# Gate products of two groups as 64-row pairs inside a burst, with stages A and B in another order

## The chip, the cores and the metric

The kernel runs on one core of one Trainium2 chip. The metric is the time in microseconds (us) of one execution on the device. A core has TensorE (PE, matmuls; PEld is its weight loads), VectorE (DVE), ScalarE (ACT), GpSimd (POOL) and SyncE (SP), each with a queue of its own that runs in order; semaphores order them among each other.

## The reference

Two layers for x of shape 4 x 12608 x 128 in f32, with 32 inducing rows and an inner width of 1024:

```python
def mab(q, kv):
    s = scale * (q @ kv.transpose(0, 2, 1))
    s = s - s.max(-1, keepdims=True)
    a = np.exp(s)
    a /= a.sum(-1, keepdims=True) + 1e-09
    return a @ kv
h = mab(I, x)                 # 32 x 128 for each batch
x = mab(x, h)                 # back to 12608 x 128
...
x_prev = x shifted by one row
xk = mu_k * x + (1.0 - mu_k) * x_prev
xr = mu_r * x + (1.0 - mu_r) * x_prev
k = np.maximum(xk @ w_k, 0.0)
v = k * k @ w_v
r = 1.0 / (1.0 + np.exp(-(xr @ w_r)))
return r * v
```

## The kernel before

The second attention ends in `a @ h`, and h has 32 rows only. So the kernel multiplies h into the weights once a batch: W is h (and h for the shifted row) times w_k, Wg the same times w_r. What goes through the big products is then R, the attention probabilities of a group of 512 rows: 32 rows for the row itself and 32 for the row before it, 64 in all. To keep f32 precision a number is split into a high and a low part; a product takes three terms (high x high, low x high, high x low). R holds both parts, and its 64 rows stand twice, in the upper and the lower half of the 128 partitions.

The work is 4 batches of 25 groups (24 of 512 rows, one of 320), and 4 units of 256 inner columns for each group: 400 steps, numbered n. The order on every engine is written out by hand:

- In each even step PE runs a burst: `up` for units n and n+1, twelve 64-row matmuls (L788) into two tiles `ps_a`. Two neighbouring matmuls use the upper and the lower 64 rows of the array.
- `square` of unit n: DVE takes the relu out of PSUM (`k_t`, L798), ACT squares it into `kh` (L803) and again into `k_t` (L804), POOL forms `kl`, the difference (L806). In the steps of the set `high_vector` DVE makes kh (L800).
- `down` of unit n-4: six 128-row matmuls (L817) into the bank `ps_v` of the group.
- `zgate` once a group, in the step of its second unit: two 128-row matmuls (L776) of Wg, whose high part lies in the upper 64 rows and whose low part lies in the lower 64, with R; then ACT's Sigmoid into `rT` (L778). The product lies in the same bank into which `down` will write v of that group.
- `gate` multiplies v with rT on DVE (L822), `store` transposes (L833) and writes out.

Between these steps stand two other stages, for which `at(n, f)` puts f at the end of step n and `soon(n, f)` puts it ahead of that step's `square`. They come in segments of 12 steps that start at s:

- Stage A, the first attention of the next batch, for one block of 2048 rows: `load_x` (1 MB to `xb`, L202), four transposes `btr` on DVE (L339) whose result SP spreads to `xt`, `scores` on PE into bank pb_a (L367), maxima, `expo` on ACT (L403, L404, result e1t), `etrans` on DVE, `hmm` on PE into pb_a (L436), `acc` on DVE.
- Stage B, the second attention of this batch, for four groups: `scores` on PE into pb_b (L617), transposes, maximum, Exp on ACT (L634), normalisation, `high` and `low` into `hl`. SP then spreads hl to the R of each group (L584, L597, L591). R has five buffers.

PSUM has eight banks: four for the two `ps_a` tiles, two for `ps_v`, and pb_a and pb_b. Sigmoid and Exp lie in two tables of ACT, and a change between them is an ACT_TABLE_LOAD. SP issues all these DMAs, in one order.

Of the kernel before, what the change touches and what calls it, by code (L numbers as in the profile page):

```python
# [19 lines left out]
def kernel(  # L20
# [38 lines left out]
    r_pool = ctx.enter_context(tc.tile_pool(name="r_pool", bufs=NR))  # L59
    mp = ctx.enter_context(tc.tile_pool(name="mp", bufs=2))  # L60
    pa = ctx.enter_context(tc.tile_pool(name="pa", bufs=2, space=bass.MemoryType.PSUM))
    pv = ctx.enter_context(tc.tile_pool(name="pv", bufs=2, space=bass.MemoryType.PSUM))
    pb = ctx.enter_context(tc.tile_pool(name="pb", bufs=1, space=bass.MemoryType.PSUM))
    banks = iter("ab" * 64)

    def pb_tile(bank=None):

# [141 lines left out]
    def stage_a_head(j):  # L209
# [32 lines left out]
                        nc.gpsimd.tensor_copy(out=S.xs[h + i][:, 1:], in_=dst[:, :G - 1])  # L242

        def scores():
            L.s1 = pv.tile([P, G], F32, name="ps_v")
            for i in range(Q):
                nc.tensor.matmul(out=L.s1[M * i:M * (i + 1), :w], lhsT=indT, rhs=S.xt[j, i][:, :w],
                                 start=True, stop=True)
# [72 lines left out]
    def stage_a(b, j, at, t):  # L321
# [131 lines left out]
            S.xb.pop(j)  # L453

        for c in range(Q):
            at(t + ((-1, 0, 1, 3) if (b, j) != (1, 0) else (4, 5, 6, 7))[c], lambda c=c: btr(c))
        if tail:
            at(t + 8, t_tr)
            soon(t + 11, t_scores)
        at(t + 9, scores)  # L460
        at(t + 10 + tail, common)
        at(t + 11 + tail, running)
        soon(t + 15, expo)
        at(t + 16, etrans)
        if tail:
            at(t + 16, t_etrans)
        at(t + 17, sums)
        at(t + 17, lambda: hmm(0))
        at(t + 17, lambda: hmm(1))
        at(t + 17, t_hmm)  # L470
        at(t + 19, acc)
        k = order_a.index((b, j))
        for bn, jn in order_a[k + 1:]:
            if jn < NBLK - 1:
                at(2 if (b, j) == (1, 0) else t + 8, lambda: load_x(bn, jn))
                if jn == NBLK - 2:
                    at(t + 8, lambda: load_x(bn, jt))
                break


    def combine(b, at=None, t=0):
# [45 lines left out]
        def hfin():  # L527
            ps = pb_tile("b")
            nc.tensor.matmul(out=ps[:, :M], lhsT=S.acc, rhs=L["sw"], start=True, stop=True)
            S.hT = sm.tile([P, M], F32, name="hT")  # L530
            nc.vector.tensor_copy(out=S.hT, in_=ps[:, :M])
            h4 = L["h4"] = sm.tile([P, Q, M], F32, name="h4", bufs=1)
            for n, mu in enumerate((muk, omuk, mur, omur)):
                nc.vector.tensor_scalar(out=h4[:, n, :], in0=ps[:, :M], scalar1=mu, scalar2=None, op0=ALU.mult)
            S.W = [wp.tile([P, F // 2], F32R, name=f"W{s}") for s in range(2)]
            S.Wg = wp.tile([P, C], F32R, name="Wg")

        def wpart(gate, tile):


            X = {}
            cw = C if gate else F // 2
            rows = slice(HP if gate else 0, P)

            def prod():
                X["ps"] = tile()[:, :cw]
                chunks = wk_sb.rearrange("p (c e d) -> p e c d", e=2, d=P)
                for n in range(Q):
                    o = X["ps"][M * n:M * (n + 1), :]
                    if not gate:  # L550
                        o = o.rearrange("m (c d) -> m c d", d=P)
                    nc.tensor.matmul(out=o, lhsT=L["h4"][:, 2 * gate + n % 2, :],  # L552
                                     rhs=wr_sb if gate else chunks[:, n // 2], start=True, stop=True)

            def high():
                nc.scalar.copy(out=(S.Wg if gate else S.W[0]), in_=X["ps"])

            def low():
                hi, lo = (S.Wg, S.Wg) if gate else S.W
                nc.vector.tensor_tensor(out=lo[rows], in0=X["ps"][rows], in1=hi.bitcast(F32)[rows],  # L560
                                        op=ALU.subtract)
            return prod, high, low

        if ahead:
# [193 lines left out]

    NG = (NBLK - 1) * Q + 1
    UB = NG * NU  # L760

    class Group:
        def __init__(self, b, g):
# [3 lines left out]
            self.ps = {}  # L767
            self.v = None

        def zgate(self):  # L770

            S, w = self.S, self.w
            R = S.R[self.g]
            ps = self.v = pv.tile([P, G], F32, name="ps_v")[:, :w]
            for s in range(2):
                nc.tensor.matmul(out=ps[:, :w], lhsT=S.Wg, rhs=R[:, s, :w], start=(s == 0), stop=(s == 1))  # L776
            self.rT = mp.tile([P, G], F32, name="rT")[:, :w]
            nc.scalar.activation(out=self.rT, in_=ps[:, :w], func=AF.Sigmoid)  # L778

        def up(self, u):  # L780

            S, w = self.S, self.w
            R = S.R[self.g]
            ps = self.ps[u] = pa.tile([P, UC, G], F32, name="ps_a")
            for n, (a, k) in enumerate(((0, 0), (1, 0), (0, 1))):
                for r in range(2):
                    rows = slice(HP * r, HP * (r + 1))
                    nc.tensor.matmul(out=ps[:, r, :w], lhsT=S.W[a][rows, u * P:(u + 1) * P],  # L788
                                     rhs=R[rows, k, :w], start=(n == 0), stop=(n == 2))
# [17 lines left out]
                                                       in1=kh.bitcast(F32)[:, :, a:z], op=ALU.subtract)  # L807

        def down(self, u):
            w = self.w  # L810
            if self.v is None:
                self.v = pv.tile([P, G], F32, name="ps_v")[:, :w]
            kh, kl = self.h.pop(u)
            for n, (wt, kk) in enumerate(((wvh, kh), (wvl, kh), (wvh, kl))):
                for c in range(UC):
                    fc = u * UC + c
                    nc.tensor.matmul(out=self.v, lhsT=wt[:, fc, :], rhs=kk[:, c, :],  # L817
                                     start=(fc == 0 and n == 0), stop=(fc == FC - 1 and n == 2))
# [5 lines left out]
        def store(self):  # L824
# [10 lines left out]
            if g % span == span - 1 or g == NG - 1:  # L835
# [126 lines left out]
    def at(n, f):  # L962
        events.setdefault(n, []).append(f)
# [3 lines left out]

    def start():

        def bank():  # L970
            return pv.tile([P, G], F32, name="ps_v")

        wk = wpart(0, bank)
        wg = wpart(1, bank)
        (sc0, df0, ex0, nm0, turn0, hi0, lo0, idle), *rest = [stage_b_first(g) for g in range(Q)]
        run([sc0, wk[0], rest[0][0], df0, ex0, wk[1], nm0, lambda: idle(1), turn0, hi0, wk[2], lo0])
        plan = ((None, None, None, at, soon, soon, at), (at,) * 4 + (soon, soon, at), (at, at, soon, at, soon, soon, at))
        steps = ((0, 0, 0, 0, 2, 2, 2), (0, 1, 1, 2, 4, 4, 4), (4, 5, 6, 7, 8, 8, 8))
        for fs, when, ns in zip(rest, plan, steps):
            for k, (f, put, n) in enumerate(zip(fs, when, ns)):  # L980
                if put is not None:
                    put(n, f)
                elif k > 0:
                    f()
        at(0, wg[0])
        at(0, wg[1])
# [6 lines left out]
    for b in range(B):  # L993
        t = b * UB + (4 if b == 0 else 0)
        for j in range(NBLK - 1):
            s = t + SEG * j
            high_vector |= {s + 4, s + 8}
            if b + 1 < B:
                stage_a(b + 1, j, at, s)
            if b or j:  # L1000
                stage_b(b, j + 1, at, s + (1 if j != (b == 0) else -3 if b else -1))
            else:
                stage_b(b, j + 1, at, 3, direct=True, early=soon, offsets=(0, 1, 1, 1, 3, 4, 4, 4, 5, 6, 7))
        if b + 1 < B:
# [10 lines left out]
    with tc.manual_schedule():  # L1015
        head()
        start()
        for n in range(len(units) + LAG + 2):
# [5 lines left out]
            if grp is None:  # L1024
                run(late)
                late = []
            else:
                if n % 2 == 0:
                    for g, v in units[n:n + 2]:
                        g.up(v)  # L1030
                run(early.pop(n, []))
                low = grp.square(u, n in high_vector)
                run(late)
                late = []
                part = grp.w - (grp.w // 2 if n >= len(units) - 3 else 0)
# [43 lines left out]
```

## Time and profile before

| | |
|---|---|
| time, three runs | 1100.82 median (1098.99 to 1100.83) us |
| the profiled execution's own time | 1100.15 us |
| its span, first to last instruction | 1098.2 us |
| mean granted TensorE clock | 0.995 |
| HBM traffic | 28.07 MB read, 25.82 MB written, 49 GB/s |

The page of the profile lists the busy time of each engine and its share of the span, the chain of work that ended last, and the groups of instructions that took most time. "busy, mean ns of one | idle before, releaser" means: total time, mean time of one instruction, and how long the engine had been idle ahead of the group, with what ended most of that.

### The profile page before, as it was taken

The page shows a single profiled execution, that of the slowest core. Times are in us where ns is not written, and L with a number is a line of the kernel's source. Part 1 is how long each engine was busy: PE and PEld are TensorE (multiplying, and loading weights), DVE is VectorE, ACT ScalarE, POOL GpSimd, SP SyncE. Part 2 cuts the span into 40 slices and gives each one's busy share as a digit, 9 for nine tenths or more (in the row PEclk, how much of TensorE's full clock was granted, in tenths as well). Part 3 has the DMA queues.
Part 4 walks back from the last instruction along what each step waited for, and adds up shares of the span by engine and source line. Part 5 has one row for each costly group of instructions (what it writes and reads, how often), then busy time and mean ns, then how long its engine had stood idle before and what let it go on. Part 6 is the DMA issues. An engine that isn't in the chain of part 4 may idle for free.

```text
span 1098.2 us, 19347 instructions
## 1 busy us (share of the span) xinstructions
PE 1071.4 (98%) x6622; PEld 736.6 (67%) x6622; DVE 911.5 (83%) x1296; ACT 961.5 (88%) x1101; POOL 947.1 (86%) x422
## 2 busy tenths in 40 slices
PE   7889999999999999999999999999999999999997
PEld 5456666666676666666676666666767667667775
DVE  4799899997788999997779899998777788887665
ACT  5487989898999898998899888989999999999995
POOL 2278988898889988989888989889888999999996
PEclk9999999999999999999999999999999999999998
DMA  9305676674156566665245746765315434433422
GB/s 276 120 5 114 159 157 163 130 167 100 27 119 163 121 161 148 136 151 121 46 81 132 173 94 152 167 145 116 72 26 116 88 60 90 94 80 68 92 36 35
DMA packets 267633, 123.59 MB, mean 113 GB/s; under 512 B 225648, under 2 KB 247056, under 8 KB 265232
## 3 DMA queue, kind: packets, MB, share of 16 engines
q1 hardware_dynamic: 267200, 122.35, 50.8%
q8 instruction: 52, 0.85, 0.3%
q14 instruction: 45, 0.37, 0.1%
q10 hardware_dynamic: 336, 0.02, 0.0%
HBM read 28.07 MB, written 25.82 MB: 49 GB/s over the span
## 4 chain that ended last, share of the span: by engine, by line
PE 89%; DVE 3%; ACT 3%; SPq 2%; issue 1%; DMA 1%; POOL 0%; DVEq 0%; ACTq 0%
PE ps_v L817 51%; PE ps_a L788 27%; PE ps_v L776 4%; PE pb_b L617 2%; PE pb_a L367 2%; PE pb_a L436 2%; DVE k_t L798 1%; ACT kh L803 1%; SPq L188 1%; SPq L95 1%; ACT k_t L804 1%; SPq L207 1%; DMA xb<-in_x_dram 1%; ACT L778 0%; PE pb_a L552 0%
## 5 line engine op out<-in xcount | busy, mean ns | idle before, releaser
L806 POOL TENSOR_TENSOR kl<-k_t,kh 128x1024 fp32r<-128x1024 f32 (+2 forms) x400 | 935.5, 2380 | 109.3 <-ACT k_t L804 102.1
L798 DVE TENSOR_SCALAR k_t<-ps_a 128x1024 f32<-128x1024 f32 (+1 forms) x400 | 477.1, 1198 | 98.2 <-PE ps_a L788 76.1
L804 ACT ACTIVATE k_t<-k_t 128x1024 f32<-128x1024 f32 (+1 forms) x400 | 417.5, 1048 | 51.7 <-DVE kh L800 18.0
L803 ACT ACTIVATE kh<-k_t 128x1024 fp32r<-128x1024 f32 (+1 forms) x352 | 365.1, 1037 | 47.5 <-DVE k_t L798 45.0
L788 PE MATMUL ps_a<-R,W 64*128 64x512 f32 (+1 forms) x2400 | 331.4, 407 | 5.2 <-DVE k_t L798 4.5
L788 PEld LDWEIGHTS ps_a<-R,W 64*128 64x128 f32 x2400 | 208.7, 184 | 126.6 <-issue 49.6
L817 PE MATMUL ps_v<-kh,wvh 128*128 128x512 f32 (+1 forms) x800 | 270.4, 419 | 2.1 <-ACT rT L778 2.1
L817 PE MATMUL ps_v<-kl,wvh 128*128 128x512 f32 (+1 forms) x800 | 248.8, 392 | 1.4 <-POOL kl L806 1.2
L817 PE MATMUL ps_v<-kh,wvl 128*128 128x512 f32 (+1 forms) x800 | 248.6, 392 | 0.0
L817 PEld LDWEIGHTS ps_v<-kh,wvh 128*128 128x128 f32 x800 | 133.8, 188 | 93.0 <-issue 48.5
L817 PEld LDWEIGHTS ps_v<-kl,wvh 128*128 128x128 f32 x800 | 149.5, 188 | 36.9 <-POOL kl L806 1.5
L817 PEld LDWEIGHTS ps_v<-kh,wvl 128*128 128x128 f32 x800 | 149.7, 188 | 34.9
L822 DVE TENSOR_TENSOR oT<-ps_v,rT 128x512 f32<-128x512 f32 (+1 forms) x100 | 66.9, 669 | 18.7 <-PE ps_v L817 18.4
L833 DVE STREAM_TRANSPOSE ot<-oT 128x512 f32<-128x512 f32 x96 | 66.9, 697 | 0.0
L776 PE MATMUL ps_v<-R,Wg 128*128 128x512 f32 (+1 forms) x200 | 63.7, 400 | 0.0
L800 DVE SCALAR_TENSOR_TENSOR kh<-ps_a,k_t 128x1024 fp32r<-128x1024 f32 x48 | 58.8, 1225 | 1.7
L778 ACT ACTIVATE rT<-ps_v 128x512 f32<-128x512 f32 (+1 forms) x100 | 57.9, 579 | 0.3
L339 DVE STREAM_TRANSPOSE xs<-xb 128x512 f32<-128x512 f32 x72 | 49.9, 693 | 0.8 <-DMA xb<-in_x_dram 0.4
L776 PEld LDWEIGHTS ps_v<-R,Wg 128*128 128x128 f32 x200 | 36.7, 189 | 8.8 <-issue 0.6
L778 ACT ACT_TABLE_LOAD x31 | 39.8, 1283 | 0.6
L617 PE MATMUL pb_b<-xt,hT 128*32 128x512 f32 x184 | 24.4, 603 | 0.3 <-DVE R L749 0.3
L663 DVE TENSOR_TENSOR hl<-pb_b,hl 128x512 fp32r<-128x512 f32 x23 | 15.8, 688 | 7.0 <-ACT hl L660 6.7
(215 smaller groups left out, 530.2 us busy)
## 6 DMA issues: line engine op xcount, KB each, us to landing
out_dram<-ot SPq DMA_DIRECT2D x184, 128.0 KB, 2.7
R<-R SPq DMA_DIRECT2D x88, 256.0 KB, 3.0
xb<-in_x_dram SPq DMA_DIRECT2D x18, 1024.0 KB, 5.4
xt<-xs SPq DMA_DIRECT2D x288, 64.0 KB, 2.0
R<-hl SPq DMA_DIRECT2D x96, 128.0 KB, 2.3
R<-hl SPq DMA_DIRECT2D x96, 127.8 KB, 2.4
kh<-in_x_dram SPq DMA_DIRECT2D x4, 512.0 KB, 8.1
kl<-in_x_dram SPq DMA_DIRECT2D x4, 512.0 KB, 7.4
```

The costliest lines, as they stand in the source:

```text
L339: nc.vector.transpose(out=xs.rearrange("p (s q) -> p s q", q=M), in_=S.xb[j][:, :, M * c:M * (c + 1)])
L776: nc.tensor.matmul(out=ps[:, :w], lhsT=S.Wg, rhs=R[:, s, :w], start=(s == 0), stop=(s == 1))
L778: nc.scalar.activation(out=self.rT, in_=ps[:, :w], func=AF.Sigmoid)
L788: nc.tensor.matmul(out=ps[:, r, :w], lhsT=S.W[a][rows, u * P:(u + 1) * P], rhs=R[rows, k, :w], start=(n == 0), stop=(n == 2))
L798: nc.vector.tensor_scalar(out=k, in0=ps, scalar1=0.0, scalar2=None, op0=ALU.max)
L800: nc.vector.scalar_tensor_tensor(out=kh, in0=ps, scalar=0.0, in1=k, op0=ALU.max, op1=ALU.mult)
L803: nc.scalar.activation(out=kh, in_=k, func=AF.Square)
L804: nc.scalar.activation(out=k, in_=k, func=AF.Square)
L806: return lambda eng, a, z: eng.tensor_tensor(out=kl[:, :, a:z], in0=k[:, :, a:z], in1=kh.bitcast(F32)[:, :, a:z], op=ALU.subtract)
L817: nc.tensor.matmul(out=self.v, lhsT=wt[:, fc, :], rhs=kk[:, c, :], start=(fc == 0 and n == 0), stop=(fc == FC - 1 and n == 2))
L822: nc.vector.tensor_tensor(out=self.oT, in0=self.v, in1=self.rT, op=ALU.mult)
L833: nc.vector.transpose(out=ot[:, o:o + w], in_=self.oT)
```

## The change

The gate products of two groups are made together. `zpair` stands in the steps n with n mod 8 = 6 from n = 14 on, behind the `up` burst, and issues six 64-row matmuls: for each of the three terms one for the first group, with the upper 64 rows, and one for the second, with the lower 64. For that Wg becomes two tiles of 128 rows, one for each part. The second matmul of a pair must write another bank than the first. The first group's product goes into the `ps_v` bank that the second group's v will use, the second group's into pb_a, or pb_b at every place where n-4 is 10 more than a segment's start (counted from the batch's start, in the first three batches). The two sigmoids come at the end of the step's work on ACT. Groups 0 and 1 keep a gate product each of its own, now with three matmuls.

Stage A and B move so that the bank is free between their own uses. In stage A the `btr` go from steps -1, 0, 1, 3 of the segment to -6, -5, -2, -1; `expo`, `etrans`, `hmm` and `acc` come two steps earlier; `load_x` goes from step 8 to step 3. Stage B always starts at s-1 (before: at s+1, with s-3 and s-1 at the starts of batches). The steps of `high_vector` change.

```diff
-        def zgate(self):
-            S, w = self.S, self.w
-            R = S.R[self.g]
-            ps = self.v = pv.tile([P, G], F32, name="ps_v")[:, :w]
-            for s in range(2):
-                nc.tensor.matmul(out=ps[:, :w], lhsT=S.Wg, rhs=R[:, s, :w], start=(s == 0), stop=(s == 1))
-            self.rT = mp.tile([P, G], F32, name="rT")[:, :w]
-            nc.scalar.activation(out=self.rT, in_=ps[:, :w], func=AF.Sigmoid)
+        def zpart(self, ps, a, k, rows, n):
+            nc.tensor.matmul(out=ps, lhsT=self.S.Wg[a][rows, :], rhs=self.S.R[self.g][rows, k, :self.w],
+                             start=(n == 0), stop=(n == len(TERMS) - 1))
+        def sigmoid(self, ps):
+            self.rT = mp.tile([P, G], F32, name="rT")[:, :self.w]
+            nc.scalar.activation(out=self.rT, in_=ps, func=AF.Sigmoid)
+        def zgate(self):
+            ps = self.bank()
+            for n, (a, k) in enumerate(TERMS):
+                self.zpart(ps, a, k, slice(0, HP), n)
+            self.sigmoid(ps)
...
+    def zpair(n, two):
+        last = two[1].b == B - 1 and two[1].g == NG - 1
+        r = n - (0 if n >= UB else 4)
+        spot = r % UB
+        side = "b" if r < (B - 1) * UB and spot < 7 * SEG and spot % SEG == SEG - 2 else "a"
+        ps = [pb_tile("b") if last else pv_tile(two[1].b * NG + two[1].g), pb_tile(side)]
+        ps = [t[:, :grp.w] for grp, t in zip(two, ps)]
+        for m, (a, k) in enumerate(TERMS):
+            for h in range(2):
+                two[h].zpart(ps[h], a, k, slice(HP * h, HP * (h + 1)), m)
+        return lambda: run([lambda grp=grp, t=t: grp.sigmoid(t) for grp, t in zip(two, ps)])
...
         for c in range(Q):
-            at(t + ((-1, 0, 1, 3) if (b, j) != (1, 0) else (4, 5, 6, 7))[c], lambda c=c: btr(c))
+            at(t + ((-6, -5, -2, -1) if b > 1 or j > 1 else (-1, 0, 1, 3) if j else (4, 5, 6, 7))[c], lambda c=c: btr(c))
...
-        soon(t + 15, expo)
-        at(t + 16, etrans)
+        soon(t + 13, expo)
+        at(t + 14, etrans)
...
-        at(t + 17, lambda: hmm(0))
-        at(t + 17, lambda: hmm(1))
+        at(t + 15, lambda: hmm(0))
+        at(t + 15, lambda: hmm(1))
...
-                at(2 if (b, j) == (1, 0) else t + 8, lambda: load_x(bn, jn))
+                at(2 if (b, j) == (1, 0) else t + 3, lambda: load_x(bn, jn))
...
-            high_vector |= {s + 4, s + 8}
+            high_vector |= {s + 2, s + (3 if (s + 2) % (2 * NU) == NU + 2 else 7)}
...
-                stage_b(b, j + 1, at, s + (1 if j != (b == 0) else -3 if b else -1))
+                stage_b(b, j + 1, at, s - 1, early=soon, offsets=(0, 1, 1, 2, 3, 5, 5, 6, 7, 7, 9))
...
+                sig = None
+                if n % (2 * NU) == NU + 2 and n > 2 * NU:
+                    sig = zpair(n, (units[n - NU - 2][0], units[n - 2][0]))
...
-                if n >= 2 * NU and u == 1:
-                    grp.zgate()
+                if sig:
+                    sig()
```

The rows below are the program's order on one engine: source line, operation, output tile <- inputs, shape, and a count where equal rows follow each other. A name's number tells one use of a buffer from the next.

PE before, in the two steps at whose end stage A's `hmm` stands: the gate product is between the two `down`, in the bank of its own group.

```order
L817 MATMUL ps_v_4624<-kh_4595,wvh_111 128x512 x2
L817 MATMUL ps_v_4624<-kh_4595,wvl_112 128x512 x2
L817 MATMUL ps_v_4624<-kl_4596,wvh_111 128x512 x2
L776 MATMUL ps_v_4753<-R_4198,Wg_3481 128x512 x2
L817 MATMUL ps_v_4624<-kh_4618,wvh_111 128x512 x2
L817 MATMUL ps_v_4624<-kh_4618,wvl_112 128x512 x2
L817 MATMUL ps_v_4624<-kl_4619,wvh_111 128x512 x2
L436 MATMUL pb_a_4770<-xb_4110,e1_4743 32x128 x16
```

PE in the changed kernel, steps 126 and 127, from the last row of the burst to `hmm`.

```order
L803 MATMUL ps_a_4728<-R_4269,W0_3509 128x512 x2
L781 MATMUL ps_v1_4735<-R_4241,Wg0_3511 128x512
L781 MATMUL pb_a_4736<-R_4269,Wg0_3511 128x512
L781 MATMUL ps_v1_4735<-R_4241,Wg1_3512 128x512
L781 MATMUL pb_a_4736<-R_4269,Wg1_3512 128x512
L781 MATMUL ps_v1_4735<-R_4241,Wg0_3511 128x512
L781 MATMUL pb_a_4736<-R_4269,Wg0_3511 128x512
L830 MATMUL ps_v0_4688<-kh_4606,wvh_111 128x512 x2
L830 MATMUL ps_v0_4688<-kh_4606,wvl_112 128x512 x2
L830 MATMUL ps_v0_4688<-kl_4607,wvh_111 128x512 x2
...
L441 MATMUL pb_a_4777<-xb_4026,e1_4761 32x128 x16
```

The gate products have moved out of the `down` stretch into the burst, and one of them lies in pb_a, which is the bank of `hmm` too.

ACT before, around the same place: stage A's Exp (L403, L404), the squares of the steps, stage B's Exp (L634), and the sigmoid.

```order
L403 ACT_TABLE_LOAD
L403 ACTIVATE alpha_4686<-mkr_4177,nb_4562 128x1
L404 ACTIVATE e1t_4684,ss_4685<-pb_a_4508,nb_4562 128x512
L803 ACTIVATE kh_4690<-k_t_4689 128x1024
L804 ACTIVATE k_t_4689<-k_t_4689 128x1024
L804 ACTIVATE k_t_4730<-k_t_4730 128x1024
L634 ACTIVATE s2_4681<-s2_4681 128x512
L803 ACTIVATE kh_4747<-k_t_4746 128x1024
L804 ACTIVATE k_t_4746<-k_t_4746 128x1024
L778 ACT_TABLE_LOAD
L778 ACTIVATE rT_4756<-ps_v_4753 128x512
```

ACT in the changed kernel, steps 125 to 127.

```order
L408 ACT_TABLE_LOAD
L408 ACTIVATE alpha_4701<-mkr_4239,nb_4647 128x1
L409 ACTIVATE e1t_4699,ss_4700<-pb_a_4580,nb_4647 128x512
L818 ACTIVATE kh_4705<-k_t_4704 128x1024
L819 ACTIVATE k_t_4704<-k_t_4704 128x1024
L637 ACTIVATE s2_4696<-s2_4696 128x512
L819 ACTIVATE k_t_4744<-k_t_4744 128x1024
L786 ACT_TABLE_LOAD
L786 ACTIVATE rT_4751<-ps_v1_4735 128x512
L786 ACTIVATE rT_4753<-pb_a_4736 128x512
```

Between stage A's Exp and the sigmoids one pair of squares less stands there than before, and two sigmoids follow each other.

SP before, at a load of x: the spread of one group (L584, L597), the load (L202), the output (L840).

```order
L591 DMA R_5081<-R_5081 64x1024
L584 DMA R_5208<-hl_4866 32x2x1
L597 DMA R_5208<-hl_4866 32x1024
L597 DMA R_5208<-hl_4866 32x2x511
L202 DMA xb_5243<-in_x_dram 128x2048
L840 DMA out_0_dram<-ot_5136 32x32x32 x4
L591 DMA R_5208<-R_5208 64x1024
```

SP in the changed kernel, step 139.

```order
L594 DMA R_5038<-R_5038 64x1024
L587 DMA R_5172<-hl_4883 32x2x1
L600 DMA R_5172<-hl_4883 32x1024
L600 DMA R_5172<-hl_4883 32x2x511
L207 DMA xb_5176<-in_x_dram 128x2048
L594 DMA R_5172<-R_5172 64x1024
L347 DMA xt_5272<-xs_5276 32x512
```

The load again stands behind a spread, but the transposes whose results SP spreads (L347) now follow it directly.

More of the change, by code (lines that the diff above doesn't have):

```diff
@@ L61, with pv_tile @@
     pa = ctx.enter_context(tc.tile_pool(name="pa", bufs=2, space=bass.MemoryType.PSUM))
-    pv = ctx.enter_context(tc.tile_pool(name="pv", bufs=2, space=bass.MemoryType.PSUM))
+    pv = ctx.enter_context(tc.tile_pool(name="pv", bufs=1, space=bass.MemoryType.PSUM))
     pb = ctx.enter_context(tc.tile_pool(name="pb", bufs=1, space=bass.MemoryType.PSUM))
     banks = iter("ab" * 64)
+    sides = iter((0, 1) * 16)
+    def pv_tile(side=None):
+        return pv.tile([P, G], F32, name=f"ps_v{next(sides) if side is None else side % 2}")
     def pb_tile(bank=None):
@@ L244, in scores @@
         def scores():
-            L.s1 = pv.tile([P, G], F32, name="ps_v")
+            L.s1 = pv_tile()
             for i in range(Q):
@@ L462, in stage_a @@
         at(t + 11 + tail, running)
-        soon(t + 15, expo)
-        at(t + 16, etrans)
+        soon(t + 13, expo)
+        at(t + 14, etrans)
         if tail:
-            at(t + 16, t_etrans)
-        at(t + 17, sums)
-        at(t + 17, lambda: hmm(0))
-        at(t + 17, lambda: hmm(1))
-        at(t + 17, t_hmm)
-        at(t + 19, acc)
+            at(t + 14, t_etrans)
+        at(t + 15, sums)
+        at(t + 15, lambda: hmm(0))
+        at(t + 15, lambda: hmm(1))
+        at(t + 15, t_hmm)
+        at(t + 17, acc)
         k = order_a.index((b, j))
@@ L535, in hfin @@
             S.W = [wp.tile([P, F // 2], F32R, name=f"W{s}") for s in range(2)]
-            S.Wg = wp.tile([P, C], F32R, name="Wg")
+            S.Wg = [wp.tile([P, C], F32R, name=f"Wg{s}") for s in range(2)]
         def wpart(gate, tile):
@@ L542, in wpart @@
             cw = C if gate else F // 2
-            rows = slice(HP if gate else 0, P)
             def prod():
@@ L555, in high @@
             def high():
-                nc.scalar.copy(out=(S.Wg if gate else S.W[0]), in_=X["ps"])
+                nc.scalar.copy(out=(S.Wg if gate else S.W)[0], in_=X["ps"])
             def low():
-                hi, lo = (S.Wg, S.Wg) if gate else S.W
-                nc.vector.tensor_tensor(out=lo[rows], in0=X["ps"][rows], in1=hi.bitcast(F32)[rows],
-                                        op=ALU.subtract)
+                hi, lo = S.Wg if gate else S.W
+                nc.vector.tensor_tensor(out=lo, in0=X["ps"], in1=hi.bitcast(F32), op=ALU.subtract)
             return prod, high, low
@@ L760 @@
     UB = NG * NU
+    TERMS = ((0, 0), (1, 0), (0, 1))
     class Group:
@@ L768, in __init__, with bank @@
             self.v = None
-        def zgate(self):
-            S, w = self.S, self.w
-            R = S.R[self.g]
-            ps = self.v = pv.tile([P, G], F32, name="ps_v")[:, :w]
-            for s in range(2):
-                nc.tensor.matmul(out=ps[:, :w], lhsT=S.Wg, rhs=R[:, s, :w], start=(s == 0), stop=(s == 1))
-            self.rT = mp.tile([P, G], F32, name="rT")[:, :w]
-            nc.scalar.activation(out=self.rT, in_=ps[:, :w], func=AF.Sigmoid)
+        def bank(self):
+            if self.v is None:
+                self.v = pv_tile(self.b * NG + self.g)[:, :self.w]
+            return self.v
+        def zpart(self, ps, a, k, rows, n):
[4 more added lines that the diff above has]
+            nc.scalar.activation(out=self.rT, in_=ps, func=AF.Sigmoid)
+        def zgate(self):
+            ps = self.bank()
+            for n, (a, k) in enumerate(TERMS):
+                self.zpart(ps, a, k, slice(0, HP), n)
+            self.sigmoid(ps)
         def up(self, u):
@@ L784, in up @@
             ps = self.ps[u] = pa.tile([P, UC, G], F32, name="ps_a")
-            for n, (a, k) in enumerate(((0, 0), (1, 0), (0, 1))):
+            for n, (a, k) in enumerate(TERMS):
                 for r in range(2):
@@ L809, in down @@
         def down(self, u):
-            w = self.w
-            if self.v is None:
-                self.v = pv.tile([P, G], F32, name="ps_v")[:, :w]
+            self.bank()
             kh, kl = self.h.pop(u)
@@ L968, in start @@
     def start():
[L970 to L974, printed above, removed]
+        wk = wpart(0, pv_tile)
+        wg = wpart(1, pv_tile)
         (sc0, df0, ex0, nm0, turn0, hi0, lo0, idle), *rest = [stage_b_first(g) for g in range(Q)]
```

## The prediction

> **What bounds the kernel now.** I read the page's busy times first, then the chain that ended last, then the costliest groups.
>
> ```profile
> PE 1071.4 (98%) x6622; PEld 736.6 (67%) x6622; DVE 911.5 (83%) x1296; ACT 961.5 (88%) x1101; POOL 947.1 (86%) x422
> PE 89%; DVE 3%; ACT 3%; SPq 2%; issue 1%; DMA 1%; POOL 0%; DVEq 0%; ACTq 0%
> L776 PE MATMUL ps_v<-R,Wg 128*128 128x512 f32 (+1 forms) x200 | 63.7, 400 | 0.0
> xb<-in_x_dram SPq DMA_DIRECT2D x18, 1024.0 KB, 5.4
> ```
>
> PE is busy 98% of the span and carries 89% of the chain; the 200 gate products are a PE group of their own. But ACT, POOL and DVE are at 83 to 88%. The next view, busy time by windows (us, then PE, PEld, DVE, ACT, POOL with counts, the granted clock, DMA share), shows the steady state and three windows of the start.
>
> ```profile
> 371.00:403.00 32.00, 32.00 (x200) 21.68 (x200) 29.92 (x43) 28.81 (x33) 28.44 (x13) 1.00 0.51 107
> 55.00:60.00 5.00, 3.59 (x27) 2.26 (x24) 4.38 (x8) 4.13 (x7) 3.42 (x2) 0.73 0.00 0
> 60.00:65.00 5.00, 4.25 (x30) 1.89 (x32) 4.36 (x8) 4.94 (x6) 3.69 (x2) 0.93 0.00 0
> ```
>
> In steady state PE never stops while ACT, at 28.81 of 32 us, has only a tenth to spare. So a PE slot saved is time saved, and work on ACT that PE is made to wait for is time lost. The timeline of PE gives the price of a slot.
>
> ```profile
> 387.50 1.67 PE L788 MATMUL ps_a<-R,W 64*128 64x512 f32 x12
> ...
> 392.10 1.66 PE L788 MATMUL ps_a<-R,W 64*128 64x512 f32 x12
> 393.69 0.73 PE L817 MATMUL ps_v<-kh,wvh 128*128 128x512 f32 x2
> ...
> 394.73 0.63 PE L817 MATMUL ps_v<-kl,wvh 128*128 128x512 f32 x2
> 395.19 0.63 PE L776 MATMUL ps_v<-R,Wg 128*128 128x512 f32 x2
> 395.66 0.63 PE L817 MATMUL ps_v<-kh,wvh 128*128 128x512 f32 x2
> ...
> 397.15 1.08 PE L436 MATMUL pb_a<-xb,e 128*32 128x128 f32 x32
> 398.16 1.67 PE L788 MATMUL ps_a<-R,W 64*128 64x512 f32 x12
> ```
>
> From burst to burst a pair of steps takes 4.60 us (387.50 to 392.10). Two 128-row matmuls advance PE by 0.47 (395.19 to 395.66), so a slot is 0.233. The burst's twelve 64-row matmuls advance it by 1.59 (392.10 to 393.69): six slots, 1.40, and 0.19 for the change of shape. So two 64-row matmuls on the two halves of the rows share one slot. Stage A's sum, `hmm`, takes 1.0 (397.15 to 398.16).
>
> **1. The pairs on PE.** A pair issues six 64-row matmuls, three slots, in place of four: 0.233 saved. It stands behind the burst in the same shape, so no change of shape is added. Of 49 pairs, 45 save 0.233 and four with a 320-column group about 0.06 (such a matmul taken at 320/512 of a slot): 10.7. Groups 0 and 1 go alone with three matmuls for two: +0.47. Together **-10.2**. LDWEIGHTS (21.68 of 32 us) run beside PE.
>
> **2. `hmm` behind the second sigmoid.** At nine places (n = 30, 54, 78, 126, 150, 174, 214, 238, 262) a pair and stage A's `hmm` fall into one pair of steps, and both write pb_a. The pair's product in pb_a must wait until Exp has read stage A's scores there, and `hmm`, at the end of step n+1, until the second sigmoid has read the product. Both are work of ACT. Its rows at such a place before, in the order that stays:
>
> ```profile
> 389.84 1.06 ACT L803 ACTIVATE kh<-k_t 128x1024 fp32r<-128x1024 f32 x1 [0.47 <-DVE k_t L798]
> 391.00 1.06 ACT L804 ACTIVATE k_t<-k_t 128x1024 f32<-128x1024 f32 x1
> 392.08 1.28 ACT L403 ACT_TABLE_LOAD   x1
> 393.37 0.29 ACT L403 ACTIVATE alpha<-mkr,nb 128x1 f32<-128x1 f32 x1
> 393.57 0.67 ACT L404 ACTIVATE e1t<-pb_a,nb 128x512 f32<-128x512 f32 x1
> 394.24 1.04 ACT L803 ACTIVATE kh<-k_t 128x1024 fp32r<-128x1024 f32 x1
> 395.37 2.25 ACT L804 ACTIVATE k_t<-k_t 128x1024 f32<-128x1024 f32 x2
> 397.53 0.61 ACT L634 ACTIVATE s<-s 128x512 f32<-128x512 f32 x1
> ...
> 400.52 1.28 ACT L778 ACT_TABLE_LOAD   x1
> 401.82 0.60 ACT L778 ACTIVATE rT<-ps_v 128x512 f32<-128x512 f32 x1
> ```
>
> Let T0 be the start of the burst of step n-2 (387.50 here). ACT takes kh of that step at T0+2.34, when DVE's relu has come, and is then busy without a gap: kh 1.16, k 1.08, table load 1.29, alpha 0.20, e1t 0.67 (ends T0+6.74), kh 1.13, k 1.08, stage B's Exp 0.65, k 1.08 (its kh is on DVE), table load 1.30, and the two sigmoids 0.49 and 0.60: the second ends at T0+13.1. PE gets to the product at T0+4.60+1.40 = 6.00 and waits 0.74 for e1t. Without any wait it would be at `hmm` at T0+2x4.60+0.70 = 9.90. It stands there until 13.1: 3.2 us a place in all, the 0.74 within it, **+28.5**. Before, nobody waited for the sigmoid (its bank was read next by the gate); that was its cover. The bounds are nought, if ACT ran ahead by that much, and 9x4.5 = 40 if a 1.3 us table load more came in. I take the chain, since each link is a row and ACT has no gap in it.
>
> **3. Stage B's scores behind the second sigmoid.** Where the product is in pb_b (n = 14, 38, 62, 110, 134, 158, 222, 246), B's scores follow at the end of step n+1. The sigmoid ends 2.34+1.16+1.08+0.49+0.60 = 5.67 after the step's burst starts; PE is there at 4.60+0.70 = 5.30: 0.4 each. At n = 86 and 182 the scores are in the same step and wait about 0.9. Together **+4.8** (0 to 10).
>
> **4. The x block behind a later spread.** SP issues everything in order. Its rows and waits:
>
> ```profile
> 405.91 0.53 SPq L202 DMA_DIRECT2D xb<-in_x_dram  x1
> 406.54 0.64 SPq L584 DMA_DIRECT2D R<-R  x1
> 412.40 1.22 SPq L597 DMA_DIRECT2D R<-hl  x2
> SPq L584 <- PE ps_a L788: 45.5, 18, 5.3
> ```
>
> With five R buffers, the spread of group f waits for the last matmul that reads R of group f-5, and already did so for up to 5.3 us. That was `up` at step 4(f-5)+2; for an even f-5 it is now the pair's product at 4(f-5)+6. SP is blocked there, and all behind it. At n = 43, 139, 227 and 251 the load of x, now at s+3, stands behind such a spread, and the first transpose, now at six steps before the next segment, needs it. From the burst T3 of that step: product ends T3+2.4, three issues (0.64+1.22) to T3+4.3, landing 5.4, T3+9.7. Then DVE, in order:
>
> ```profile
> 392.20 0.70 DVE L339 STREAM_TRANSPOSE xs<-xb 128x512 f32<-128x512 f32 x1
> ...
> 394.00 1.21 DVE L798 TENSOR_SCALAR k_t<-ps_a 128x1024 f32<-128x1024 f32 x1
> 395.24 1.23 DVE L800 SCALAR_TENSOR_TENSOR kh<-ps_a,k_t 128x1024 fp32r<-128x1024 f32 x1
> ```
>
> Behind the transpose (0.62 to the next start) are the relu of the next step (1.24) and its kh on DVE (1.14): T3+12.7. The second half of the next burst writes the PSUM tile that this kh reads, and PE is there at T3+5.30+0.80 = 6.1. It waits 6.6 us, four times: **+26.4**. The bounds are nought, if the spread is not what holds the load, and 4x8 = 32 with a landing at 6.8. I take 6.6: the wait on R is in the row above already. Elsewhere the load waits for `hmm` alone and lands about 1.5 us before its transpose, so I cost it at nothing; it is covered by those 1.5 us.
>
> **5. The clock.** The chip's start shows what idle PE can cost: in the windows above the granted clock is 0.73 and 0.93, after this wait:
>
> ```profile
> 56.74 1.22 PE L788 MATMUL ps_a<-R,W 64*128 64x512 f32 x6 [1.41 <-DVE k_t L798]
> 35.00:40.00 5.00, 3.34 (x61) 1.61 (x53) 3.68 (x15) 2.70 (x9) 0.48 (x2) 1.00 0.00 0
> ```
>
> The loss is 5x0.27+5x0.07 = 1.7 us. A window with as much idle time (1.66 of 5 us, in pieces) kept 1.00, so not every wait does it. I take one such loss for each of the four long waits, **+6.8** (0, to 13 losses, 22). The Trainium skill (TensorE: Matmul & The Clock Gate, Part 1: The HAM clock gate) says that the clock halves after at least one idle free-running window of about 3.4 us. By that rule waits of 3.2 us or less never fill a window and those of 6.6 may; an estimate from that page is up to 3.4 us at half clock, 1.7 each, the same sum. The row speaks against it as far as it goes: there the clock fell after 1.41 us idle, so the short waits could trigger it too.
>
> The other moves (stage A's Exp and transposes two to five steps earlier, `acc`, which steps have kh on DVE) leave the counts on every engine as they were; table loads are as many as before. They fill the same 29.92 of 32 us on DVE, and I cost them at nothing; without that cover a DVE operation of 0.7 us at each of 18 segments would be 13.
>
> **The sum.** -10.2 + 28.5 + 4.8 + 26.4 + 6.8 = +56.3. On the profiled execution (1100.15, of which 1098.2 is the span) that gives 1156.4; the median shown is 0.7 above it, so **1157**.
>
> **The rivals.** (a) The blocked loads cost nothing, since the spread is released earlier or DVE has time: -26.4-6.8, 1123.5. For it: the longest wait of a spread was 5.3 us and hurt nobody. Against: the load moves from behind two segments' slack to six steps ahead of its use. (b) The clock falls after all 13 waits: 9x1.7 = 15 more, 1172. For it the row with 1.41 us; against it the window that kept 1.00. (c) The other side: ACT is ahead. ACT's tenth to spare gathers between the places, PE's waits are covered, and only the slots count: 1100.8-10.2 = 1090.6. It decides once the waits total under 10.2 us, that is, under 0.8 at each of 13 places, for which ACT would have to end its sigmoid 2.4 us sooner. Against it: ACT cannot start before DVE's relu of the same burst (the row with 0.47 idle), so what it has to spare cannot be saved up. (d) No change: gains and waits cancel within 0.2% (2.2 us, about the least that a measurement of this kernel tells from no change); only by accident.
>
> **How the numbers follow.** The full sum, with terms 2 to 4 each off by up to a third (1140 to 1168): 0.58. Rival (a), 1116 to 1132: 0.17. Rival (b): 0.06. Between 1103 and 1116, half of term 2 only: 0.04. Rival (c): 0.12. Same: 0.03. The full sum and (a) hold 0.75 between 1116 and 1168; with the upper part of the half case and the lower edge of (b), 1110 to 1170 holds about 0.79. Faster 0.12, same 0.03, slower 0.85.
>
> **What would show it.** Profile after: the gate products as 300 matmuls with 64 rows on PE (step 1); PE idle ahead of `hmm` for ACT's second rT, and ahead of the product in pb_a for e1t (step 2); ahead of B's scores for rT (3); SP waiting at the spread for a product, DVE's transpose idle for the DMA of xb, then PE's burst idle for DVE's kh (4); windows with a clock below 1.00 (5). The prediction is wrong if PE's idle time ahead of `hmm` is under 1 us a place, or if no transpose waits for xb.

## The result and the profile after

The changed kernel takes 1197.1 us against 1100.0 in the same runs: a ratio of 1.0874 (95% interval 1.0852 to 1.0895). One of the four executions behind this median took 2011.0 us and stands outside the ratio; the median of the other three is 1196.0. The direction was forecast and the size was not: +56 forecast, +97 measured, above the range.

Busy times and the chain of the page, after:

```profile
PE 1094.1 (91%) x6722; PEld 739.6 (62%) x6722; DVE 908.6 (76%) x1296; ACT 967.3 (81%) x1101; POOL 947.9 (79%) x422
PE 54%; ACT 14%; DVE 13%; issue 7%; DMA 4%; SPq 2%; POOL 1%; DVEq 0%; ACTq 0%
```

DVE, ACT and POOL are busy as long as before, to within 6 us. PE's share of the chain fell from 89 to 54%. PE's idle time is 1196.5-1094.1 = 102.4 us, before 1098.2-1071.4 = 26.8: 75.6 more. Its busy time grew by 22.7, though each pair saves a slot. So the 98.3 us that the span grew by are waits and slower matmuls. PE's waits by what ended them (us in total, times, longest):

```profile
PE ps_a L803 <- DVE kh L815: 38.7, 9, 7.4
PE pb_a L441 <- ACT rT L786: 19.6, 9, 2.9
PE pb_a L781 <- ACT e1t L409: 4.6, 9, 0.9
PE pb_b L620 <- ACT rT L786: 3.3, 10, 0.8
```

None of these four is in the list of before. They are the waits of the prediction's steps 4, 2, 2 and 3; the counts of 9 and 10 are those of steps 2 and 3, and the first came nine times where step 4 had four. On SP, the spread's waits were 45.5 us for `up` before; now the list has, for the pair's product:

```profile
SPq L587 <- PE pb_a L781: 159.9, 25, 11.7
```

**A pair and `hmm` on one bank** (n = 30), timelines of PE and ACT:

```profile
144.07 1.67 PE L803 MATMUL ps_a<-R,W 64*128 64x512 f32 x12
...
146.36 0.49 PE L781 MATMUL pb_a<-R,Wg 64*128 64x512 f32 x1 [0.39 <-ACT e1t L409]
...
147.25 0.73 PE L830 MATMUL ps_v<-kh,wvh 128*128 128x512 f32 x2
...
152.33 1.30 PE L441 MATMUL pb_a<-xb,e 128*32 128x128 f32 x32 [2.01 <-ACT rT L786]
```

```profile
145.55 0.67 ACT L409 ACTIVATE e1t<-pb_a,nb 128x512 f32<-128x512 f32 x1
...
149.90 1.28 ACT L786 ACT_TABLE_LOAD   x1
151.19 0.60 ACT L786 ACTIVATE rT<-ps_v 128x512 f32<-128x512 f32 x1
151.68 0.59 ACT L786 ACTIVATE rT<-pb_a 128x512 f32<-128x512 f32 x1
```

ACT ends the second sigmoid at 152.27, and 0.06 later PE starts `hmm`. The burst that T0 names began at 139.48, so the sigmoid ends at T0+12.8 (forecast 13.1).

**The load of x behind a spread** (n = 43 to 49): SP, DVE, PE.

```profile
193.35 0.67 SPq L587 DMA_DIRECT2D R<-hl  x1
194.07 1.27 SPq L600 DMA_DIRECT2D R<-hl  x2
195.38 0.58 SPq L207 DMA_DIRECT2D xb<-in_x_dram  x1
```

```profile
201.05 0.71 DVE L344 STREAM_TRANSPOSE xs<-xb 128x512 f32<-128x512 f32 x1 [6.96 <-issue]
201.69 1.19 DVE L813 TENSOR_SCALAR k_t<-ps_a 128x1024 f32<-128x1024 f32 x1
202.98 1.23 DVE L815 SCALAR_TENSOR_TENSOR kh<-ps_a,k_t 128x1024 fp32r<-128x1024 f32 x1
```

```profile
190.96 1.66 PE L803 MATMUL ps_a<-R,W 64*128 64x512 f32 x12
192.46 0.39 PE L781 MATMUL ps_v<-R,Wg 64*128 64x512 f32 x1
...
193.26 0.73 PE L830 MATMUL ps_v<-kh,wvh 128*128 128x512 f32 x2
...
196.26 0.96 PE L803 MATMUL ps_a<-R,W 64*128 64x512 f32 x6
204.26 1.65 PE L803 MATMUL ps_a<-R,W 64*128 64x512 f32 x6 [7.04 <-DVE kh L815]
```

The pair of step 46 starts at 192.46, the spread goes out at 193.35, the load at 195.38; the transpose starts at 201.05 after 6.96 us of DVE idle, and PE's second half of the burst stands for 7.04. The profile names no releaser for the transpose ("issue"); a load lands 5.6 us after its issue in the median, which is 201.0 here. The same rows show the price of a pair: from burst to burst 190.96 to 196.26 is 5.30, that is 0.70 above the 4.60 without one, as forecast.

### The profile page after: what moved, and what is told of

The parts are those of the page before. It is cut to its first block, busy times and chain, and to the rows that moved or that the text cites. A ratio compares the mean times of both kernels' runs of the same rounds, so it can differ in the third digit from the quotient of the medians.

```text
span 1196.5 us, 19640 instructions
## 1 busy us (share of the span) xinstructions
PE 1094.1 (91%) x6722; PEld 739.6 (62%) x6722; DVE 908.6 (76%) x1296; ACT 967.3 (81%) x1101; POOL 947.9 (79%) x422
## 4 chain that ended last, share of the span: by engine, by line
PE 54%; ACT 14%; DVE 13%; issue 7%; DMA 4%; SPq 2%; POOL 1%; DVEq 0%; ACTq 0%
PE ps_v L830 30%; PE ps_a L803 18%; DVE k_t L813 8%; ACT kh L818 4%; ACT k_t L819 4%; DMA xb<-in_x_dram 3%; PE pb_b L620 2%; ACT rT L786 2%; PE pb_a L441 1%; ACT L786 1%; PE pb_a L372 1%; DVE kh L815 1%; PE ps_v L781 1%; DVE xs L344 1%; ACT e1t L409 1%
## 5 line engine op out<-in xcount | busy, mean ns | idle before, releaser
L803 PE MATMUL ps_a<-R,W 64*128 64x512 f32 (+1 forms) x2400 | 346.1, 417 | 48.3 <-DVE kh L815 38.7
L803 PEld LDWEIGHTS ps_a<-R,W 64*128 64x128 f32 x2400 | 213.0, 190 | 179.3 <-issue 46.5
L830 PE MATMUL ps_v<-kh,wvh 128*128 128x512 f32 (+1 forms) x800 | 275.4, 426 | 3.2 <-ACT rT L786 2.9
L830 PE MATMUL ps_v<-kh,wvl 128*128 128x512 f32 (+1 forms) x800 | 252.2, 397 | 0.0
L830 PEld LDWEIGHTS ps_v<-kl,wvh 128*128 128x128 f32 x800 | 151.9, 191 | 35.7
L781 PE MATMUL ps_v<-R,Wg 64*128 64x512 f32 (+1 forms) x150 | 45.5, 398 | 0.0
L441 PE MATMUL pb_a<-xb,e 128*32 128x128 f32 x576 | 20.4, 284 | 20.4 <-ACT rT L786 19.6
L781 PE MATMUL pb_a<-R,Wg 64*128 64x512 f32 (+1 forms) x114 | 33.0, 396 | 4.6 <-ACT e1t L409 4.6
L441 PEld LDWEIGHTS pb_a<-xb,e 128*32 128x32 f32 x576 | 14.8, 110 | 27.7 <-ACT rT L786 23.5
L375 DVE TENSOR_REDUCE mx<-pb_a 128x1 f32<-128x512 f32 x18 | 12.4, 691 | 24.6 <-PE pb_a L372 24.2
```

What stands on the lines that cost most here:

```text
L781: nc.tensor.matmul(out=ps, lhsT=self.S.Wg[a][rows, :], rhs=self.S.R[self.g][rows, k, :self.w], start=(n == 0), stop=(n == len(TERMS) - 1))
```

## Experiments

Ratios are to the kernel before, with 95% intervals. Where no other kernel is named, the diff is against the changed kernel.

| kernel | us | ratio |
|---|---|---|
| e1, spreads behind the pair | 1156.8 | 1.0509 (1.0491 to 1.0527) |
| e2, transposes back | 1155.7 | 1.0503 (1.0476 to 1.0530) |
| e3, no second product at nine places | 1168.8 | 1.0632 (1.0598 to 1.0666) |
| e4, order alone | 1123.0 | 1.0205 (1.0190 to 1.0220) |
| e5, sigmoids first | 1178.3 | 1.0720 (1.0689 to 1.0752) |
| e6, order, transposes back | 1120.8 | 1.0194 (1.0176 to 1.0211) |
| e7, bank free | 1139.7 | 1.0363 (1.0347 to 1.0380) |
| e8, bank free, sigmoids first | 1127.9 | 1.0249 (1.0235 to 1.0263) |
| e9, balanced | 1105.2 | 1.0047 (1.0031 to 1.0063) |
| e10, order, balanced | 1157.7 | 1.0517 (1.0500 to 1.0533) |
| e11, order, one switch | 1142.8 | 1.0394 (1.0377 to 1.0412) |
| e12, order, both Exps in a step | 1137.5 | 1.0340 (1.0315 to 1.0365) |
| e13, order, Exp apart | 1097.8 | 0.9989 (0.9977 to 1.0000) |

**e1: is it the spread that holds the load?**

```diff
-            s = max(first + ..., NU * (f - NR) + 3 + (0 if full else i))
+            free = NU * (f - NR) + (3 if (f - NR) % 2 or f - NR < 2 else 7)
+            s = max(first + ..., free + (0 if full else i))
```

> The changed kernel with the spread of a group that reuses the R buffer of the first group of a pair put four steps later, behind that pair's product. Theory (a spread in front of the load of x waits for the pair): the four waits of 7.2 to 7.6 us at n = 48, 144, 232, 256 shrink to the 2 us that the other late loads show, 4x5.4 = 21.6, and part of the lost clock with it, about 5: 1170 (1163 to 1180). Rival (SP is behind with its own issues, the spread's wait matters little): 1190 or more.

Measured 1156.8, 40 us less than the changed kernel. PE's waits:

```profile
PE pb_a L441 <- ACT rT L787: 19.5, 9, 2.9
PE ps_a L804 <- DVE kh L816: 10.3, 5, 4.3
```

The four long waits are gone, not merely shortened to 2 us, and so are those of 1.92 and 1.71 us at n = 60 and 244; the wait at n = 24 grew from 3.27 to 4.30. The clock came back in part (0.975 to 0.986), and the time is below the expected range. The wait at `hmm` is untouched. The rival is out.

**e2: only the transposes at their old steps.**

```diff
-            at(t + ((-6, -5, -2, -1) if b > 1 or j > 1 else (-1, 0, 1, 3) if j else (4, 5, 6, 7))[c], ...
+            at(t + ((-1, 0, 1, 3) if (b, j) != (1, 0) else (4, 5, 6, 7))[c], ...
```

> The changed kernel with only the four transposes of each x block back at the old steps (-1, 0, 1, 3 of the segment in place of -6, -5, -2, -1). Theory (DVE's first transpose waits for the block, and PE for DVE): all ten waits of PE ahead of the second half of a burst go, 45 us, with some 12 us of lost clock; the waits for the sigmoid stay: 1140 (1133 to 1148). Rival (DVE is crowded by the new order of stage B, and PE waits for its relus): the transposes fall on stage B's steps now, 1165 or more.

Measured 1155.7, between the two forecasts. The waits for x go, but DVE's work, crowded, brings new ones:

```profile
PE pb_a L441 <- ACT rT L786: 21.5, 9, 2.9
PE pb_a L441 <- DVE e L420: 5.0, 6, 0.8
...
PE ps_a L803 <- DVE kh L815: 2.9, 2, 1.5
```

Both theories hold in part: 36 us of waits for kh went, and 4 for DVE's e came (5.0 against 0.8).

**e3: the nine second products left out** (the second group's gate is taken from the first group's product there).

> The changed kernel, which at the nine places where the pair and hmm both use pb_a leaves the second group's product out and takes its sigmoid from the first group's product; the two sigmoids stay. Theory (PE waits there for ACT to read the bank): 21 + 9 us of waits go, some 8 us of lost clock, and 4 us at n = 60 and 244 where the load waited for a late hmm: 1155 (1148 to 1165). Rival (the wait only moves, to DVE's transpose or the gate): 1180 or more.

```profile
PE ps_a L803 <- DVE kh L815: 39.4, 9, 9.3
PE ps_a L803 <- DVE k_t L813: 11.6, 12, 3.9
PE ps_v L830 <- ACT rT L786: 7.5, 11, 1.5
```

Measured 1168.8; the profiled execution took 1175.2. Both pb_a waits are gone, as the theory says, but the gain is 28 us and not 42. The waits at n = 60 and 244, which the theory put down to a late `hmm`, did not go: they grew from 1.92 to 3.89 and from 1.71 to 3.00, and that at n = 144 from 7.45 to 9.29. Those for relu and rT grew as well. So the wait at `hmm` had been cover for later ones.

**e5: the sigmoids ahead of the step's squares**, the one line `sig()` moved up.

> The changed kernel with the two sigmoids of a pair ahead of the squares of their step on ACT in place of behind them; nothing else. Theory (PE stands at hmm for ACT's order of work): each sigmoid ends one square (1.06 us) sooner where kh is on DVE, two where it is on ACT, so 9x1.06 at hmm and the 4.2 us ahead of stage B's scores go, with some lost clock; the waits for x stay: 1182 (1175 to 1189). Rival (PE waits for something else that ends with the sigmoid): 1194 or more.

```profile
PE pb_a L441 <- ACT rT L786: 8.7, 9, 1.1
```

Measured 1178.3, in the range. The wait at `hmm` fell from 19.6 to 8.7, 1.2 a place, for one square taken out of its way (forecast 1.06); the wait ahead of stage B's scores is no longer listed. It is ACT's order that PE stands for.

**e4, e6: the new order with the old gate products.** e4 is the kernel before with the change's steps; e6 has the transposes back as well.

> The kernel before with only the new order of stages A and B (steps, high_vector, load of x) and its old gate products. Theory (the order costs only where a load of x is late, and without pairs no spread holds it for long): six to ten waits of about 2 us, some lost clock: 1118 (1106 to 1130). Rival (the order as such is the loss, the pairs cost nothing): 1170 or more.

> The kernel before with the new order of stages A and B, but with the transposes of x at their old steps. Theory (the order costs by late loads of x alone): as before, 1101 (1098 to 1105). Rival (the new steps of stage B and of kh on DVE crowd DVE): 1108 or more.

e4 lies in its range and e6 does not: with the transposes back it is 2 us faster and not 22. PE's waits for kh fell from 12.4 to 6.7, and 6.1 for DVE's e came. I had missed that without pairs the old sigmoid at s+1 falls between the two Exps of a segment. The groups of ACT in e4:

```profile
L778 ACT ACT_TABLE_LOAD x46 | 59.0, 1283 | 0.8
L634 ACT ACT_TABLE_LOAD x27 | 34.6, 1283 | 0.5
```

The sigmoid's line has 46 table loads, where it had 31 before, and stage B's Exp 27, where it had 13. Neither kernel is a clean test of the order.

**e10, e11, e12: three attempts at a clean one, each with a wait of its own.**

> The kernel before with the new order of stages A and B, old gate products, the same spread of DVE's work as e9_balanced, and each sigmoid one step later, so that it falls behind both Exps of a segment (without that the new order has 92 table loads in the program in place of 62, as e4 and e6 have). Theory (the order costs by DVE's crowding, late loads and those table loads only): 1101 (1098 to 1106). Rival (the new steps of stage B cost in themselves): 1112 or more.

> The kernel of e4_order_alone with each sigmoid one step later, which takes its 30 additional table loads away (38 us of ACT); transposes, loads and kh on DVE as the change has them. Theory (e4's 22 us are late loads and DVE): 1117 (1110 to 1122). Rival (they are ACT's table loads): 1106 or less.

> The kernel before, old gate products and sigmoids where they were; stage B two steps earlier as in the change, the spread of DVE's work of e9_balanced, and stage A's Exp in the step of stage B's Exp, so that the table loads stay at 62. Theory (stage B's place as such costs nothing; what e4, e6, e10 and e11 lost is late loads, DVE, table loads and the sigmoids that e10 and e11 put late): 1101 (1098 to 1105). Rival (B at s-1 costs in itself): 1110 or more. With it, e9 says what the pairs are worth when nothing waits for them: theory, e9 within 5 us of this.

The waits of PE that decide, of e10 and of e12:

```profile
PE ps_v L822 <- ACT rT L783: 44.5, 30, 3.7
```

```profile
PE ps_a L788 <- DVE k_t L798: 28.9, 22, 2.4
```

In e10 and e11 the later sigmoid holds the bank that the group's first `down` writes. In e12 DVE's etrans stands behind an Exp of the same step (DVE's list: 43.8 us at 18 places for e1t), and the relus behind it come late. All three missed their ranges.

**e13: e12 with etrans two steps after its Exp.**

> The kernel of e12_order_both_exps with the transpose of stage A's exponentials (etrans) two steps after its Exp, as before the change, in place of in the same step, where DVE waited 2.4 us for ACT in each segment. Theory (that wait is e12's loss, and stage B's place costs nothing in itself): 1102 (1098 to 1107). Rival (stage B at s-1 costs in itself): 1115 or more.

Measured 1097.8, ratio 0.9989: no difference that is clear of noise. Stage B at s-1 costs nothing in itself, where DVE's work is spread as in e9. Stage A's `etrans`, `hmm` and `acc` are at their old steps here, so no run shows the change's whole order without pairs and without a wait of its own. What is left of PE's waits for DVE:

```profile
PE ps_a L788 <- DVE k_t L798: 3.1, 7, 1.0
```

**e7, e8, e9: pairs without the waits.** e7 frees the bank and the load; e8 adds the sigmoids first; e9 spreads DVE's work.

```diff
+            free = NU * (f - NR) + (3 if (f - NR) % 2 or f - NR < 2 else 7)
...
-            at(t + ((-6, -5, -2, -1) if b > 1 or j > 1 ...
+            at(t + ((-1, 0, 1, 3) ...
-        soon(t + 13, expo)
+        soon(t + 12 + tail, expo)
...
-        at(t + 15, lambda: hmm(0))
+        h = t + (17 if (t + 14) % (2 * NU) == NU + 2 else 15)
+        at(h, lambda: hmm(0))
...
-                at(2 if (b, j) == (1, 0) else t + 3, lambda: load_x(bn, jn))
+                at(2 if (b, j) == (1, 0) else t + 8, lambda: load_x(bn, jn))
# e9, against e8
-            at(t + ((-1, 0, 1, 3) ...
+            at(t + ((2, 3, 4, -2) ...
-                at(2 if (b, j) == (1, 0) else t + 8, lambda: load_x(bn, jn))
+                at(2 if (b, j) == (1, 0) else t + 6, lambda: load_x(bn, jn))
-            high_vector |= {s + 2, s + (3 if (s + 2) % (2 * NU) == NU + 2 else 7)}
+            high_vector |= {s + 6, s + 8}
```

> The changed kernel with the pairs as they are, and: transposes of x at their old steps, the load of x at step 8 again, spreads of R behind the pair that still reads the buffer, stage A's Exp one step sooner, and hmm and acc two steps later in the segments whose pair falls on step 2. Theory (all of the loss is the three waits; without them 10.2 us of slots remain as gain, less about 8 for the waits at n = 86, 96, 182, 192, 270, 288 and ahead of stage B's scores): 1097 (1092 to 1103). Rival (the loads, transposes and spreads only collide elsewhere, or pairs cost PE more than three slots): 1110 or more.

> The kernel of e7_bank_free with the sigmoids of a pair ahead of their step's squares. Theory: the 2.3 us ahead of stage B's scores go, and part of the waits at n = 86 and 182: 1094 (1089 to 1100). Rival (kh and k come later by two sigmoids, PE waits for POOL's kl four steps on): above e7_bank_free by 2 or more.

> The kernel of e8_bank_free_sigmoids_first with DVE's work spread: the transposes of an x block at steps -2, 2, 3, 4 of its segment (there: -1, 0, 1, 3), kh on DVE at steps 6 and 8 (there: 2 and 3, or 2 and 7), the load of x at step 6. Theory (what is left in e8 is DVE behind by up to 2 us in steps -1 to 3 of each segment, 20 us of PE waits with 5 to 10 of lost clock): 1101 (1093 to 1108). Rival (ACT or a late load takes DVE's place): 1115 or more.

PE's waits in e7, and then the first of e9's list with e9's busy times:

```profile
PE ps_a L805 <- DVE kh L817: 13.5, 9, 1.7
PE pb_a L441 <- DVE e L420: 5.1, 6, 0.8
```

```profile
PE ps_a L805 <- DVE k_t L815: 7.1, 14, 1.4
```

```profile
PE 1069.2 (97%) x6722; PEld 726.0 (66%) x6722; DVE 907.6 (82%) x1296; ACT 962.0 (87%) x1101; POOL 946.4 (86%) x422
```

e7 and e8 missed their ranges: with x and the bank out of the way, DVE's lateness became the wait. e8's sigmoids brought 11.8 us against e7, more than forecast, and its rival did not come. e9 takes DVE's lateness away too and is at 1105, in its range: of the 97 us, 92 are gone with the pairs left in. It is still 0.5% slower than before, and 7.4 us slower than e13, which has no pairs and DVE's work spread in the same way (the expectation at e12 was 5 us at most). The two differ in stage A's steps too, so this is no price of the pairs alone; but no kernel with pairs here gained anything.

## Why the prediction was wrong

The span grew by 98.3 us where the sum had 56.3. The 42.0 that are missing are 18.1 of slower matmuls (24.9 for the 6.8 of step 5), 15.9 of waits (75.6 for the 59.7 of steps 2 to 4) and 8.0 of slots that were not saved (2.2 for the 10.2 of step 1).

- **Step 1, the pairs: per pair right, as a sum not shown.** A pair costs 0.70 and saves 0.233. But in e9, with the changed kernel's 6722 matmuls and little waiting, PE is busy 1069.2 us, 2.2 below before (1071.4) and 4.0 below e13 (1073.2), where the step had 10.2. No run separates where the rest went, so that is open.
- **Step 2: right.** From the burst at 144.07 to `down` at 147.25 is 3.18 us, where the pair without a wait (190.96 to 193.26) takes 2.30: 0.88 late. From `down` to `hmm` is 5.08, and 3.46-0.47 = 2.99 before (393.69 to 397.15, less the gate product): 2.09 late. Together 2.97 at this place; forecast 3.2. PE's idle at all nine is 19.6+4.6 = 24.2, and e3 and e5 show the mechanism. "Before, nobody waited for the sigmoid" was not quite so: the list of before has three such waits of PE, 2.1 us in all.
- **Step 3: right** in its ten places; 3.3 us of idle against 4.8 forecast.
- **Step 4: the step that failed first.** The four places are those forecast, at 7.0 to 7.5 us in place of 6.6, and e1 shows that the spread did it. The sentence "Elsewhere the load waits for `hmm` alone and lands about 1.5 us before its transpose" was wrong. At n = 24, 60, 108, 120, 208 and 244 PE waits 3.27, 1.92, 0.37, 0.99, 2.71 and 1.71, 11.0 in all (those at 60, 108 and 244 stand in the list under DVE's k_t). What holds the load is SP's own queue, here ahead of n = 60:

```profile
216.86 0.50 SPq L594 DMA_DIRECT2D R<-R  x1
223.88 0.64 SPq L587 DMA_DIRECT2D R<-hl  x1
224.56 1.27 SPq L600 DMA_DIRECT2D R<-hl  x2
225.93 2.44 SPq L347 DMA_DIRECT2D xt<-xs  x4
228.47 2.48 SPq L853 DMA_DIRECT2D out_dram<-ot  x4
230.99 0.64 SPq L594 DMA_DIRECT2D R<-R  x1
231.72 1.52 SPq L587 DMA_DIRECT2D R<-hl  x1
233.29 1.27 SPq L600 DMA_DIRECT2D R<-hl  x2
234.66 0.53 SPq L207 DMA_DIRECT2D xb<-in_x_dram  x1
```

  SP issued nothing from 217.36 to 223.88, when the pair's product of n = 54 let the spread go, and then had fifteen issues, most of about 0.6 us, ahead of the load. `hmm` started at 229.1 and the load went out 5.5 us after that. At n = 60 and 244 this is the blocked spread once more, at one remove: e1, which moves spreads alone, took these two waits away with `hmm` as late as before. The lateness of `hmm` is not the cause, since in e3, where `hmm` does not wait, both grew. The other four stay in e1 (4.30, 1.02, 0.95 and 2.14); at n = 24 eight issues stand ahead of the load, from 112.58 to 118.51, while `hmm` had ended at 113.4. The cover of 1.5 us was counted without the queue's issues, which the prediction does not name.
- **Step 5: the term that was most mis-sized.** Forecast 6.8. The same 6722 matmuls keep PE busy 1094.1 us here and 1069.2 in e9: 24.9 us of slower matmuls, at a mean clock of 0.975 against 0.995. The trace's record of the clock has half clock in pieces of 3.41 us, 17 of them ahead of PE's last work, where the kernel before has one. A piece costs the 1.7 us of the forecast, but there were 16 more where it had four: nine belong to the four long waits, two or three each, six follow waits at `hmm` (n = 30, 78, 126, 150, 174 and 214), and two follow the waits at n = 24 and 208. At 1.7 each, 16 are 27 us, of which a part falls where PE stands anyway. That this is near rival (b)'s 22, whose chance I gave as 0.06, is in part luck: (b) had one loss behind each of 13 waits. Two places with the same wait of 2.0 us at `hmm` (n = 30, the first two rows, and n = 54, the next three), cut at the ends of the pieces, then the longest wait (n = 144):

```profile
149.64:153.05 3.41, 1.40 (x31) 0.91 (x34) 2.10 (x3) 3.38 (x5) 3.41 (x2) 1.00 1.16 191
153.05:156.46 3.41, 3.41 (x29) 1.98 (x17) 1.14 (x1) 0.17 (x1) 2.52 (x2) 0.50 1.01 234
224.73:228.14 3.41, 2.33 (x11) 1.53 (x9) 2.99 (x4) 3.38 (x5) 2.91 (x2) 1.00 0.54 118
228.14:231.55 3.41, 2.48 (x44) 1.86 (x44) 1.08 (x2) 1.82 (x3) 3.33 (x2) 1.00 0.88 156
231.55:234.96 3.41, 3.41 (x16) 2.46 (x16) 3.34 (x6) 2.38 (x3) 1.14 (x2) 1.00 0.78 152
484.00:488.00 4.00, 3.53 (x11) 2.40 (x12) 4.00 (x6) 2.19 (x3) 2.35 (x1) 0.50 0.54 120
488.00:492.00 4.00, 4.00 (x17) 2.38 (x15) 1.08 (x2) 2.99 (x3) 2.90 (x3) 0.63 0.76 140
```

- **The moves that I costed at nothing** (DVE's kh and transposes). They do cost once the transposes are put back (e2: 5.0 us for e; e7: 13.5 for kh and 5.1 for e). In the changed kernel they show at n = 104 and 304 alone, 1.46 us of PE each: there no load is late, and at 104 DVE has its kh twice in a row. Elsewhere the longer waits seem to cover them. The prediction's "without that cover [...] 13" was of that order.

The waits came to 75.6 us of idle more, where steps 2 to 4 had 59.7. The other loads added 11.0 and the four long waits 2.4 (28.8 for 26.4); steps 2 and 3 took 5.8 less than forecast; the 8.3 that remain are small waits elsewhere. Rival (a), that the blocked loads cost nothing, is ruled out by e1 and the waits for x. Rival (c), that ACT is ahead, is ruled out by `hmm` starting 0.06 us after the sigmoid.

## What to carry to other kernels

Where an instruction moves a product to another bank, or a load to an earlier step, write down the whole in-order queue behind it on each engine, DMA issues included: here a four-step wait at one small spread held a 1 MB load, and the load held DVE and then PE; and once let go, the queue still had fifteen issues to catch up with. A wait's price should not be summed place by place as if the rest stood still: removing one wait (e3) brought 28 us for an expected 42, since other waits grew. And an experiment that moves a step makes waits of its own (e10 to e12 did), so read its waits before taking its time for a verdict.

## What the runs showed of the hardware

The granted clock fell to half (0.50 in the second of the rows by windows above) after PE had stood 2.0 us at n = 30, but not after the same wait at n = 54 (1.00). The rows show the difference: at n = 30 the wait lies within one window of 3.41 us and leaves PE 1.40 us of work there, while at n = 54 it falls on two windows with 2.33 and 2.48. Over the changed kernel's whole trace, from 9.7 us on, where the record of the clock begins: of the windows of 3.41 us at full clock, cut in this way, every one in which PE stood 1.73 us or more was followed by half clock, and none in which it stood 1.68 or less. That is about half a window; the traces of the other kernels put the border between 1.55 and 1.76. After the four waits of 7 us the clock was at 0.50 every time, and at n = 144 it was at 0.50 to 0.63 for 8 us. The prediction's row with 1.41 us was the better guide here.

The Trainium skill (TensorE: Matmul & The Clock Gate, Part 1: The HAM clock gate) has the half clock and a free-running window of about 3.4 us, and the trace agrees with both. That an idle window must pass first does not agree with the place at n = 30, where PE worked 1.40 us in the window ahead of the half clock.
